# One zeroed tile for four masks, and a selector summed by TensorE, in a decode kernel that streams 54 MB

## The chip, the cores and the metric

The kernel runs on one core of a Trainium2 chip. The metric is the device time of one execution in microseconds. Beside the time, every execution has a span: from its first to its last instruction in the profile. The difference of the two is the time outside the span. All executions quoted here are recorded as of the fast state. The three sets of experiments ran on three different chips, each with the kernel before beside it; its time outside the span was 1.97 to 1.98 us on all three, so this quantity is compared across sets. A ratio is the mean time of one kernel's fast runs over that of the other's fast runs of the same rounds, so it is not quite the ratio of the medians that are quoted beside it.

## The reference

The reference mixes two branches for one token: attention over the last 4096 cached keys of 16 key/value heads, and a gelu MLP.

```python
g = sigmoid((x * gate_w).sum(-1, keepdims=True))
a = attention(x, k_cache[..., -4096:, :], v_cache[..., -4096:, :], wq, wo)   # 32 query heads, Dh 128
b = gelu(x @ w1 + b1) @ w2 + b2                                              # 576 -> 4608 -> 576
return g * a + (1 - g) * b
```

Each weight and each cached row in the window is used once, so the kernel reads 53.6 MB for very little arithmetic.

## The kernel before

All large transfers are issued by SyncE into five big buffers, in the order w1, wq, four key tiles, two value tiles, half of w2, and the rest of the values, wo and w2. GpSimd builds small masks at the start, while the weights come in. Four of them concern us: `perm` (it permutes the query heads), `lo31` (it selects row p mod 31), and `om_t` and `wo_tail`, which must be zero where nothing is written later.

```python
perm = const.tile([P, 4, 4, 32], BF16, name="perm")
nc.gpsimd.memset(perm[:], 0.0)
nc.gpsimd.affine_select(out=perm[:], in_=perm[:], ...)
hi5 = const.tile([P, 5], FP32, name="hi5")
nc.gpsimd.memset(hi5[:], 1.0)
# ... two selects on hi5
lo31 = const.tile([P, RW], BF16, name="lo31")            # RW = 31
nc.gpsimd.memset(lo31[:], 0.0)
for a in range(5):                                       # ones where p - 31 a == r
    nc.gpsimd.affine_select(out=lo31[:], in_=lo31[:], pattern=[[-1, RW]], base=-RW * a, ...)
om_t = const.tile([P, 64], BF16, name="om_t")
nc.gpsimd.memset(om_t[:], 0.0)
wo_tail = const.tile([48, 4, D], BF16, name="wo_tail")
nc.gpsimd.memset(wo_tail[:].bitcast(FP32), 0.0)
# ... more masks, last of all qz_flat
```

Near the end the attention output of each head is scaled by the gate over the softmax sum, masked into four groups of rows (`om`) and a tail (`om_t`), and re-laid by a product with the selector:

```python
rgh = ...   # rg x gh[:, 0:4], VectorE
rgt = ...   # rg x gh[:, 4],   VectorE, one more instruction
om, om_t = o_ps * rgh, o_ps * rgt
ov_mm = nc.tensor.matmul(ov_ps[:, 0:RO], lhsT=om, rhs=lo31[:], start=True, stop=True)
ov_mm = nc.tensor.matmul(ov_ps[0:64, RO:RO+4], lhsT=om_t, rhs=lo31[:, 0:4], start=True, stop=True)
```

GpSimd's program has 63 instructions and VectorE's 63, by the count that the change goes by. The trace records 60 and 59 of them, and 2230 of TensorE's; the differences between kernels are the same in both counts.

Of the kernel before, what the change touches and what calls it, by code (L numbers as in the profile page):

```python
# [9 lines left out]
FP32 = mybir.dt.float32  # L10
BF16 = mybir.dt.bfloat16
I32 = mybir.dt.int32
ACT = mybir.ActivationFunctionType
ALU = mybir.AluOpType
# [4 lines left out]
def kernel(  # L19
# [15 lines left out]
    nc = tc.nc  # L35

    P = 128
    D = 576
    Hq, Hkv, Dh = 32, 16, 128
# [126 lines left out]
    const = ctx.enter_context(tc.tile_pool(name="const", bufs=1))  # L166
# [36 lines left out]
    for base, pattern, keep in (  # L203
# [4 lines left out]
        n = 1  # L208
# [8 lines left out]
        out=is0[:], in0=low[:], scalar1=0.0, scalar2=None, op0=ALU.is_equal  # L217
    )
    alt = is0[:, 0 : 2 * NI].rearrange("p (i t) -> p i t", t=2)
    ones = const.tile([P, P], FP32, name="ones")  # L220
    nc.gpsimd.memset(ones[:], 1.0)
    ident = const.tile([P, P], BF16, name="ident")
    make_identity(nc, ident[:])
    perm = const.tile([P, 4, 4, 32], BF16, name="perm")
    nc.gpsimd.memset(perm[:], 0.0)
    nc.gpsimd.affine_select(
        out=perm[:],
        in_=perm[:],
        pattern=[[-64, 2], [-1, 2], [0, 4], [-2, 32]],
        compare_op=ALU.not_equal,  # L230
        fill=1.0,
        base=0,
        channel_multiplier=1,
    )
    RW = 31
    hi5 = const.tile([P, 5], FP32, name="hi5")
    nc.gpsimd.memset(hi5[:], 1.0)
    nc.gpsimd.affine_select(
        out=hi5[:],
        in_=hi5[:],  # L240
        pattern=[[-RW, 5]],
        compare_op=ALU.is_ge,
        fill=0.0,
        base=0,
        channel_multiplier=1,
    )
    nc.gpsimd.affine_select(
        out=hi5[:],
        in_=hi5[:],
        pattern=[[RW, 5]],  # L250
        compare_op=ALU.is_ge,
        fill=0.0,
        base=RW - 1,
        channel_multiplier=-1,
    )
    lo31 = const.tile([P, RW], BF16, name="lo31")
    nc.gpsimd.memset(lo31[:], 0.0)
    for a in range(5):
        nc.gpsimd.affine_select(
            out=lo31[:],  # L260
            in_=lo31[:],
            pattern=[[-1, RW]],
            compare_op=ALU.not_equal,
            fill=1.0,
            base=-RW * a,
            channel_multiplier=1,
        )
    om_t = const.tile([P, 64], BF16, name="om_t")
    nc.gpsimd.memset(om_t[:], 0.0)
    wo_tail = const.tile([48, 4, D], BF16, name="wo_tail")  # L270
    nc.gpsimd.memset(wo_tail[:].bitcast(FP32), 0.0)
    c0 = 2 * NI
    hi16 = const.tile([P, 16], FP32, name="hi16")
    nc.gpsimd.tensor_scalar(
        out=hi16[:], in0=is0[:, c0 : c0 + 16], scalar1=-SCALE, scalar2=None, op0=ALU.mult
# [5 lines left out]
        out=row_of[:],  # L281
        in_=row_of[:],
        pattern=[[0, 16], [-1, HB], [0, 2]],
        compare_op=ALU.not_equal,
        fill=1.0,
        base=0,
        channel_multiplier=1,
# [4 lines left out]
        out=foreign[:],  # L292
        in_=foreign[:],
        pattern=[[0, P], [-1, HB]],
        compare_op=ALU.not_equal,
        fill=0.0,
        base=0,
        channel_multiplier=1,
# [4 lines left out]
        out=xdup.rearrange("p (d t) -> p d t", t=2),  # L303
        in_=x_row.rearrange("p (d o) -> p d o", o=1).to_broadcast([1, D, 2]),
    )
    xs_ps = ps_m.tile([P, NI, 1], FP32, name="xs_ps", tag="m")
    for i in range(NI):
        nc.tensor.matmul(  # L308
            xs_ps[:, i, :],
            lhsT=xdup[:, i : 2 * D : NI],  # L310
            rhs=one_b[0:1, 0:1],
            start=(i == 0),
            stop=(i == NI - 1),
# [4 lines left out]
        out=x2[:], in0=xs_ps[:].to_broadcast([P, NI, 2]), in1=alt, op=ALU.mult  # L318
# [5 lines left out]
        out=junk_row,  # L324
        in0=x_row,
        in1=gw_row,
        scale=1.0,
        scalar=0.0,
        op0=ALU.mult,
# [12 lines left out]
        out=omg[:], in0=g_t[:], scalar1=-1.0, scalar2=1.0, op0=ALU.mult, op1=ALU.add  # L342
# [3 lines left out]
        out=b2g[:], in0=b2_row, scalar1=omg[0:1, 0:1], scalar2=None, op0=ALU.mult  # L346
    )
    gh = const.tile([P, 1, 5], FP32, name="gh")
    nc.vector.tensor_scalar(
        out=gh[:, 0, :], in0=hi5[:], scalar1=g_t[:, 0:1], scalar2=None, op0=ALU.mult  # L350
# [22 lines left out]
    for j in range(NJ):  # L373
        nc.tensor.matmul(
            h_ps[:, j:NF:NJ],
            lhsT=b1_t[:, j:FH:NJ],
            rhs=ident[0:2, 0:2],
            start=(j == 0),
            stop=False,
# [5 lines left out]
    for i in range(NI):  # L385
        for j in range(NJ):
            nc.tensor.matmul(  # L387
                h_ps[:, j:NF:NJ],
                lhsT=w1_t[:, i, j:FH:NJ],
                rhs=x2[:, i, :],  # L390
                start=False,
                stop=(i == NI - 1 and j == NJ - 1),
# [9 lines left out]
        out=poly[:],  # L402
        in0=z2[:],
        scalar1=2.0 * C0 * 0.044715,
        scalar2=2.0 * C0,
        op0=ALU.mult,
# [11 lines left out]
        out=gt[:], in0=hacc[:], scalar=omg[:, 0:1], in1=r_t[:], op0=ALU.mult, op1=ALU.mult  # L418
# [4 lines left out]
    for i in range(NI):  # L423
        for j in range(Hq // 2):
            nc.tensor.matmul(  # L425
                q_ps[:, j : Hq : Hq // 2],
                lhsT=wq_t[:, i, j * Dh : (j + 1) * Dh],
                rhs=x2[:, i, :],
                start=(i == 0 and j == 0),
                stop=(i == NI - 1 and j == Hq // 2 - 1),  # L430
# [5 lines left out]
    for j in range(4):  # L436
        nc.tensor.matmul(
            qj_ps[:, j, :, :].rearrange("p g q -> p (g q)"),
            lhsT=perm[:, j, :, :].rearrange("p b l -> p (b l)"),
            rhs=q_b[:],  # L440
            start=True,
            stop=True,
        )
    for b in range(4):
# [6 lines left out]
            out=diag[:, :, :, 0:8],  # L451
            in_=qj_ps[quad].rearrange("p j g q -> p g j q"),
# [140 lines left out]
    for u in range(2):  # L593
        load_tail = nc.sync.dma_start(
            out=wo_tail[32 * u : 32 * u + 16].rearrange("h j n -> h (j n)"),
            in_=wo_src[16 * u : 16 * u + 16, 4 * RW : P, :].rearrange("h j n -> h (j n)"),
        )
        four_engines.append(load_tail.ins.name)
    o_ps = ps_m.tile([P, Hq, 1], FP32, name="o_ps", tag="m")

    def value_products(g):
        for c in range(NCK):
# [16 lines left out]
        out=ls[:],  # L619
        in0=same8[:, 0:8].rearrange("p (o q) -> p o q", o=1).to_broadcast([P, NG, 8]),  # L620
        in1=sums[:].to_broadcast([P, NG, 8]),
        op=ALU.mult,
# [6 lines left out]
            t_ps, lhsT=ones[:], rhs=ls[:].rearrange("p g q -> p (g q)"), start=True, stop=True  # L629
        ),  # L630
    )
    rg = const.tile([P, Hq, 1], FP32, name="rg")
    nc.vector.reciprocal(out=rg[:, :, 0], in_=t_ps)  # L633
    rgh = const.tile([P, Hq, 4], FP32, name="rgh")
    nc.vector.tensor_tensor(
        out=rgh[:],
        in0=rg[:].to_broadcast([P, Hq, 4]),
        in1=gh[:, :, 0:4].to_broadcast([P, Hq, 4]),
        op=ALU.mult,
    )  # L640
    rgt = const.tile([P, Hq], FP32, name="rgt")
    nc.vector.tensor_scalar(
        out=rgt[:], in0=rg[:, :, 0], scalar1=gh[:, 0, 4:5], scalar2=None, op0=ALU.mult
    )
    queue("pe", lambda: value_products(3))

# [1 line left out]
    RO = RW  # L648
    wo_t = big.tile([P, RO, D], BF16, name="wo_t", tag="D")
    for r0, r1 in ((0, 16), (16, RO)):  # L650
        nc.sync.dma_start(  # L651
            out=wo_t[:, r0:r1, :].rearrange("p r n -> p (r n)"),
            in_=wo_src[:, 0 : 4 * RW, :].rearrange("h (a r) n -> h a (r n)", a=4)[
                :, :, r0 * D : r1 * D
            ],
        )
    for j0, j1 in ((0, 10), (10, 16), (16, 18)):
        nc.sync.dma_start(out=w2_t[:, NJ + j0 : NJ + j1, :], in_=w2_src[:, 1, j0:j1, :])  # L658

    om = const.tile([P, Hq, 4], BF16, name="om")  # L660
    nc.vector.tensor_tensor(  # L661
        out=om[:], in0=o_ps[:].to_broadcast([P, Hq, 4]), in1=rgh[:], op=ALU.mult
    )
    with tc.issue_after(issued["pe"].ins):
        for f in range(6):
            y_add(gt[:, f : f + 1], w2_t[:, f, :])
    nc.vector.tensor_tensor(
        out=om_t[:].rearrange("p (u h) -> p u h", u=2)[:, :, 0:16],
        in0=o_ps[:, :, 0].rearrange("p (u h) -> p u h", u=2),
        in1=rgt[:].rearrange("p (u h) -> p u h", u=2),  # L670
        op=ALU.mult,
    )
    ov_ps = ps_m.tile([P, RO + 4], FP32, name="ov_ps", tag="m")
    ov_mm = nc.tensor.matmul(
        ov_ps[:, 0:RO],
        lhsT=om[:].rearrange("p h a -> p (h a)"),
        rhs=lo31[:],
        start=True,
        stop=True,
    )  # L680
    with tc.issue_after(ov_mm.ins):
        ov_mm = nc.tensor.matmul(
            ov_ps[0:64, RO : RO + 4], lhsT=om_t[:], rhs=lo31[:, 0:4], start=True, stop=True
        )
    ov = const.tile([P, RO], BF16, name="ov")
    nc.vector.tensor_copy(out=ov[:], in_=ov_ps[:, 0:RO])
    ov_tail = const.tile([48, 4], BF16, name="ov_tail")
# [46 lines left out]
```

## Time and profile before

| | before |
|---|---|
| time, median of the runs beside the change | 132.34 us |
| profiled execution: time, span, difference | 132.28, 130.28, 2.00 us |
| read from HBM | 53.62 MB |
| GpSimd's masks end at | 17.49 us |
| the 864 KB of w2 that the chain names landed at | 127.39 us |
| the last 288 KB of w2 landed at | 128.07 us |

The table is read from the bottom up: the weights that the chain names land at 127.4 us, the last products, two casts and a store take the 2.9 us that follow, and two more microseconds lie outside every instruction. The lines of the profile stand in the prediction.

### The profile page before, as it was taken

Reading aid. Unit: us, or ns where it says so; the run is one execution under the profiler, and the core shown is the slowest. Engines: PE = TensorE matmul, PEld = TensorE weight load, DVE = VectorE, ACT = ScalarE, POOL = GpSimd, SP = SyncE. Lnnn points to the kernel's source line nnn. Section 1 sums busy time; section 2 is a strip of 40 time slices with the busy share of each in tenths; the row PEclk is TensorE's granted clock in tenths of the full one; section 3 lists DMA queues with packets and bytes.
Section 4 is the critical chain, followed back from the end, with each engine's and each line's share of the span. In section 5 each row is a group of like instructions: output and inputs, shape, how many; then the busy total and the mean of one; then the engine's idle time right before and its main releaser. Section 6 shows DMA issues by size and latency. Waiting matters only on the chain.

```text
span 130.3 us, 2411 instructions
## 1 busy us (share of the span) xinstructions
PE 80.7 (62%) x1145; PEld 46.1 (35%) x1077; DVE 53.7 (41%) x49; ACT 8.3 (6%) x18; POOL 10.1 (8%) x34
## 2 busy tenths in 40 slices
PE   0036999476003998949909995985300930899973
PEld 0036949475000121202201121685300920864641
DVE  0056100300079969999999995604000020010001
ACT  3000000003000000030003003021000000000001
POOL 5029930000000000000000000000000000000000
PEclk9999999999999999999996899975555555555999
DMA  7999999899999899899999999899999999999980
GB/s 232 421 436 439 468 401 498 363 463 438 392 448 463 372 453 483 372 443 473 392 433 463 412 412 463 376 444 473 397 423 448 423 407 421 430 427 421 403 354 25
DMA packets 2508, 53.75 MB, mean 413 GB/s; under 512 B 286, under 2 KB 290, under 8 KB 580
## 3 DMA queue, kind: packets, MB, share of 16 engines
q1 hardware_dynamic: 2490, 53.61, 96.5%
q8 instruction: 8, 0.13, 0.4%
q10 hardware_dynamic: 10, 0.01, 0.0%
HBM read 53.62 MB, written 0.00 MB: 412 GB/s over the span
## 4 chain that ended last, share of the span: by engine, by line
DMA 52%; DVE 24%; PE 14%; issue 6%; SPq 2%
DMA k_t<-in_A_k_cache_dram 27%; DMA w_t<-in_B_w_dram 25%; DVE kt L494 19%; PE s_ps L516 7%; PE o_ps L603 5%; DVE m L532 3%; DVE pt L565 2%; PE y_ps L359 1%; SPq L651 1%; DVE mr L535 1%; SPq L658 0%; SPq L194 0%; PE mt_ps L541 0%; DVE out_row L702 0%; SPq L190 0%
## 5 line engine op out<-in xcount | busy, mean ns | idle before, releaser
L516 PE MATMUL s_ps<-kt,qz_flat 128*128 128x512 bf16 x128 | 32.6, 412 | 17.2 <-DVE kt L494 10.4
L494 DVE STREAM_TRANSPOSE kt<-k_t 128x4096 f32<-128x4096 f32 x8 | 35.3, 4432 | 11.7 <-DMA k_t<-in_A_k_cache_dram 10.3
L603 PE MATMUL o_ps<-pt,v_t 128*128 128x8 bf16 x512 | 14.2, 167 | 16.8 <-DMA v_t<-in_A_v_cache_dram 14.8
L516 PEld LDWEIGHTS <-qz_flat 128*128 128x128 bf16 x64 | 6.8, 107 | 40.3 <-issue 40.2
L603 PEld LDWEIGHTS <-v_t 128*128 128x128 bf16 x512 | 14.1, 102 | 17.5 <-DMA v_t<-in_A_v_cache_dram 15.1
L387 PEld LDWEIGHTS <-w_t 128*128 128x128 bf16 x162 | 10.2, 165 | 0.9 <-issue 0.9
L387 PE MATMUL h_ps<-x,w_t 128*128 128x2 bf16 x162 | 10.4, 202 | 0.0
L359 PE MATMUL y_ps<-w_t,gt 128*1 128x288 bf16 x72 | 7.2, 363 | 1.2 <-DMA w_t<-in_B_w_dram 1.2
L553 ACT ACTIVATE p_t<-s_ps,negm 128x1024 bf16<-128x1024 f32 x4 | 4.5, 1113 | 50.9 <-DVE negm L549 50.9
L633 DVE RECIPROCAL rg<-mt_ps 128x32 f32<-128x32 f32 x1 | 0.4, 358 | 15.5 <-PE mt_ps L628 15.5
L565 DVE STREAM_TRANSPOSE pt<-p_t 128x1024 bf16<-128x1024 bf16 x4 | 4.9, 1224 | 2.7 <-ACT p_t L553 2.7
L425 PE MATMUL q_ps<-x,wq_t 128*128 128x2 bf16 x144 | 4.0, 166 | 2.7 <-DMA wq_t<-in_A_wq_dram 2.7
L702 DVE CAST out_row<-y_ps 1x288 bf16<-1x288 f32 x1 | 0.4, 445 | 11.7 <-PE y_ps L359 11.7
L308 PE MATMUL xs_ps<-one_b,rows 1*128 1x1 bf16 x9 | 0.7, 195 | 7.4 <-DVE rows L302 7.4
L532 DVE TENSOR_REDUCE m<-s_ps 128x1 f32<-128x1024 f32 x4 | 4.8, 1196 | 1.1 <-PE s_ps L516 1.1
L359 PEld LDWEIGHTS <-gt 128*1 128x1 bf16 x72 | 3.7, 99 | 3.6 <-issue 1.6
L425 PEld LDWEIGHTS <-wq_t 128*128 128x128 bf16 x144 | 3.9, 104 | 2.8 <-DMA wq_t<-in_A_wq_dram 2.8
L396 DVE COPY hacc<-h_ps 128x36 f32<-128x36 f32 x1 | 0.2, 196 | 10.6 <-PE h_ps L387 10.6
L359 PE MATMUL y_ps<-wo_t,ov 128*1 128x288 bf16 x62 | 4.3, 286 | 0.2 <-DMA wo_t<-in_A_wo_dram 0.2
L661 DVE TENSOR_TENSOR om<-o_ps,rgh 128x128 bf16<-128x128 f32 x1 | 0.3, 292 | 8.8 <-PE o_ps L603 8.8
L302 DVE COPY rows<-rows 1x1152 bf16<-1x1152 bf16 x1 | 0.7, 748 | 6.5 <-DMA rows<-in_A_x_dram 6.5
L359 PEld LDWEIGHTS <-ov 128*1 128x1 bf16 x62 | 2.6, 83 | 1.8 <-issue 0.8
(77 smaller groups left out, 39.1 us busy)
## 6 DMA issues: line engine op xcount, KB each, us to landing
k_t<-in_A_k_cache_dram SPq DMA_DIRECT2D x4, 4096.0 KB, 31.8
v_t<-in_A_v_cache_dram SPq DMA_DIRECT2D x4, 4096.0 KB, 23.2
wq_t<-in_A_wq_dram SPq DMA_DIRECT2D x1, 4608.0 KB, 25.8
w_t<-in_B_w_dram SPq DMA_DIRECT2D x1, 2880.0 KB, 14.2
w_t<-in_B_w_dram SPq DMA_DIRECT2D x1, 2592.0 KB, 23.1
w_t<-in_B_w_dram SPq DMA_DIRECT2D x1, 2304.0 KB, 8.1
wo_t<-in_A_wo_dram SPq DMA_DIRECT2D x1, 2304.0 KB
wo_t<-in_A_wo_dram SPq DMA_DIRECT2D x1, 2160.0 KB
```

Of the source, the lines that this page charges most:

```text
L302: nc.vector.tensor_copy(out=xdup.rearrange("p (d t) -> p d t", t=2), in_=x_row.rearrange("p (d o) -> p d o", o=1).to_broadcast([1, D, 2]),)
L359: last = nc.tensor.matmul(y_out[s], lhsT=vec, rhs=row[:, s * DH : (s + 1) * DH], start=start, stop=stop, skip_group_check=True,)
L387: nc.tensor.matmul(h_ps[:, j:NF:NJ], lhsT=w1_t[:, i, j:FH:NJ], rhs=x2[:, i, :], start=False, stop=(i == NI - 1 and j == NJ - 1), skip_grou ...
L425: nc.tensor.matmul(q_ps[:, j : Hq : Hq // 2], lhsT=wq_t[:, i, j * Dh : (j + 1) * Dh], rhs=x2[:, i, :], start=(i == 0 and j == 0), stop=(i ...
L494: lambda: nc.vector.transpose(out=kt[g, f][:].bitcast(FP32), in_=keys.rearrange("p c d -> p (c d)").bitcast(FP32),),
L516: last = nc.tensor.matmul(s_ps[g][:, u * 512 : (u + 1) * 512].rearrange("p (c k) -> p c k", k=32), lhsT=qz(g, j, 2 * f + half), rhs=kv[:, ...
L532: queue("dve", lambda: nc.vector.reduce_max(out=m1[:], in_=s_ps[g][:], axis=AX.X))
L535: lambda: nc.vector.tensor_scalar(out=mr[:], in0=hi16[:], scalar1=m1[:, 0:1], scalar2=None, op0=ALU.mult),
L553: nc.scalar.activation(out=p_t[:].rearrange("p c k -> p (c k)"), in_=s_ps[g][:], func=ACT.Exp, bias=negm[:, 0:1], scale=SCALE, accum_out=s ...
L565: lambda: nc.vector.transpose(out=pt[:, g, :, :].rearrange("p c q -> p (c q)"), in_=p_t[:].rearrange("p c k -> p (c k)"),),
L603: last = nc.tensor.matmul(o_ps[:, 8 * g : 8 * g + 8, 0], lhsT=v_t[g][:, c, :], rhs=pt[:, g, c % 32, 8 * (c // 32) : 8 * (c // 32) + 8], st ...
L651: nc.sync.dma_start(out=wo_t[:, r0:r1, :].rearrange("p r n -> p (r n)"), in_=wo_src[:, 0 : 4 * RW, :].rearrange("h (a r) n -> h a (r n)", ...
```

## The change

Its intent is to shorten two engines' programs: GpSimd from 63 to 51 instructions, VectorE from 63 to 62. The four zeroed tiles become parts of one, so one memset serves. The five selects that filled `lo31` one after the other become one select on five separate selectors (`at31`), and TensorE adds their products up in PSUM. VectorE makes five columns of `rgh` at once instead of four and one.

```diff
-    perm = const.tile([P, 4, 4, 32], BF16, name="perm")
-    nc.gpsimd.memset(perm[:], 0.0)
+    RW = 31
+    NZ = 512 + 5 * RW + 1 + 64
+    zeros = const.tile([P, NZ + 4 * D], BF16, name="zeros")
+    nc.gpsimd.memset(zeros[:].bitcast(FP32), 0.0)
+    perm = zeros[:, 0:512].rearrange("p (j b l) -> p j b l", j=4, b=4)
+    at31 = zeros[:, 512 : 512 + 5 * RW].rearrange("p (a r) -> p a r", a=5)
+    om_t = zeros[:, NZ - 64 : NZ]
+    wo_tail = zeros[0:48, NZ : NZ + 4 * D].rearrange("p (j n) -> p j n", j=4)
 ... select on perm as before
+    nc.gpsimd.affine_select(out=at31, in_=at31, pattern=[[-RW, 5], [-1, RW]], ...)
     hi5 = const.tile([P, 5], FP32, name="hi5")
-    nc.gpsimd.memset(hi5[:], 1.0)
     nc.gpsimd.affine_select(
-        in_=hi5[:],
+        in_=ones[:, 0:5],
 ...
-    lo31, its memset and its five selects; om_t, wo_tail and their memsets
 ...
-    rgh = const.tile([P, Hq, 4], FP32, name="rgh")
+    rgh = const.tile([P, Hq, 5], FP32, name="rgh")
 ...
-    rgt and its tensor_scalar
 ...
+    ov_mm = nc.tensor.matmul(
+        ov_ps[0:64, RO : RO + 4], lhsT=om_t, rhs=at31[:, 4, 0:4], start=True, stop=True
+    )
+    for a in range(4):
+        with tc.issue_after(ov_mm.ins):
+            ov_mm = nc.tensor.matmul(
+                ov_ps[:, 0:RO],
+                lhsT=om[:].rearrange("p h a -> p (h a)"),
+                rhs=at31[:, a, :],
+                start=(a == 0),
+                stop=(a == 3),
+            )
```

More of the change, by code (lines that the diff above doesn't have):

```diff
@@ L223 @@
     make_identity(nc, ident[:])
-    perm = const.tile([P, 4, 4, 32], BF16, name="perm")
-    nc.gpsimd.memset(perm[:], 0.0)
+    RW = 31
[6 more added lines that the diff above has]
+    wo_tail = zeros[0:48, NZ : NZ + 4 * D].rearrange("p (j n) -> p j n", j=4)
     nc.gpsimd.affine_select(
-        out=perm[:],
-        in_=perm[:],
+        out=perm,
+        in_=perm,
         pattern=[[-64, 2], [-1, 2], [0, 4], [-2, 32]],
@@ L234 @@
     )
-    RW = 31
+    nc.gpsimd.affine_select(
+        out=at31,
+        in_=at31,
+        pattern=[[-RW, 5], [-1, RW]],
+        compare_op=ALU.not_equal,
+        fill=1.0,
+        base=0,
+        channel_multiplier=1,
+    )
     hi5 = const.tile([P, 5], FP32, name="hi5")
-    nc.gpsimd.memset(hi5[:], 1.0)
     nc.gpsimd.affine_select(
         out=hi5[:],
-        in_=hi5[:],
+        in_=ones[:, 0:5],
         pattern=[[-RW, 5]],
@@ L255 @@
     )
-    lo31 = const.tile([P, RW], BF16, name="lo31")
-    nc.gpsimd.memset(lo31[:], 0.0)
-    for a in range(5):
-        nc.gpsimd.affine_select(
-            out=lo31[:],
-            in_=lo31[:],
-            pattern=[[-1, RW]],
-            compare_op=ALU.not_equal,
-            fill=1.0,
-            base=-RW * a,
-            channel_multiplier=1,
-        )
-    om_t = const.tile([P, 64], BF16, name="om_t")
-    nc.gpsimd.memset(om_t[:], 0.0)
-    wo_tail = const.tile([48, 4, D], BF16, name="wo_tail")
-    nc.gpsimd.memset(wo_tail[:].bitcast(FP32), 0.0)
     c0 = 2 * NI
@@ L633 @@
     nc.vector.reciprocal(out=rg[:, :, 0], in_=t_ps)
-    rgh = const.tile([P, Hq, 4], FP32, name="rgh")
+    rgh = const.tile([P, Hq, 5], FP32, name="rgh")
     nc.vector.tensor_tensor(
         out=rgh[:],
-        in0=rg[:].to_broadcast([P, Hq, 4]),
-        in1=gh[:, :, 0:4].to_broadcast([P, Hq, 4]),
+        in0=rg[:].to_broadcast([P, Hq, 5]),
+        in1=gh[:].to_broadcast([P, Hq, 5]),
         op=ALU.mult,
-    )
-    rgt = const.tile([P, Hq], FP32, name="rgt")
-    nc.vector.tensor_scalar(
-        out=rgt[:], in0=rg[:, :, 0], scalar1=gh[:, 0, 4:5], scalar2=None, op0=ALU.mult
     )
@@ L661 @@
     nc.vector.tensor_tensor(
-        out=om[:], in0=o_ps[:].to_broadcast([P, Hq, 4]), in1=rgh[:], op=ALU.mult
+        out=om[:], in0=o_ps[:].to_broadcast([P, Hq, 4]), in1=rgh[:, :, 0:4], op=ALU.mult
     )
@@ L667 @@
     nc.vector.tensor_tensor(
-        out=om_t[:].rearrange("p (u h) -> p u h", u=2)[:, :, 0:16],
+        out=om_t.rearrange("p (u h) -> p u h", u=2)[:, :, 0:16],
         in0=o_ps[:, :, 0].rearrange("p (u h) -> p u h", u=2),
-        in1=rgt[:].rearrange("p (u h) -> p u h", u=2),
+        in1=rgh[:, :, 4].rearrange("p (u h) -> p u h", u=2),
         op=ALU.mult,
@@ L674 @@
     ov_mm = nc.tensor.matmul(
-        ov_ps[:, 0:RO],
-        lhsT=om[:].rearrange("p h a -> p (h a)"),
-        rhs=lo31[:],
-        start=True,
-        stop=True,
-    )
-    with tc.issue_after(ov_mm.ins):
-        ov_mm = nc.tensor.matmul(
-            ov_ps[0:64, RO : RO + 4], lhsT=om_t[:], rhs=lo31[:, 0:4], start=True, stop=True
-        )
+        ov_ps[0:64, RO : RO + 4], lhsT=om_t, rhs=at31[:, 4, 0:4], start=True, stop=True
+    )
+    for a in range(4):
[7 more added lines that the diff above has]
+            )
     ov = const.tile([P, RO], BF16, name="ov")
```

## The prediction

> **What bounds the kernel now.** I read the page's forty slices first, then the table by stage, then the chain that ended last, and last the timelines of the two places that the change touches: GpSimd's masks at the start, and the last 16 us.
>
> In the slices each digit of the DMA row is a busy share in tenths, and GB/s is what was moved:
>
> ```profile
> DMA  7999999899999899899999999899999999999980
> GB/s 232 421 436 439 468 401 498 363 463 438 392 448 463 372 453 483 372 443 473 392 433 463 412 412 463 376 444 473 397 423 448 423 407 421 430 427 421 403 354 25
> HBM read 53.62 MB, written 0.00 MB: 412 GB/s over the span
> ```
>
> The DMA row has no hole except at its two ends. The table by stage is sharper (each engine's busy time, then the granted clock, the DMA share and GB/s):
>
> ```profile
> 37.00:60.00 23.00, 16.31 (x66) 3.58 (x34) 21.55 (x8) 1.20 (x2) 0.00 (x0) 1.00 1.01 432
> 90.00:105.00 15.00, 6.19 (x220) 6.11 (x217) 0.00 (x0) 0.00 (x0) 0.00 (x0) 0.50 1.00 427
> 115.00:122.00 7.00, 6.81 (x64) 3.29 (x62) 0.47 (x3) 0.15 (x1) 0.00 (x0) 0.61 1.01 427
> ```
>
> The DMA share is 1.00 whether VectorE is busy nearly throughout (37 to 60 us) or idle (90 to 105 us). The queue never runs dry, so the bytes fix the end. An estimate from these rows: 53.62 MB / 430 GB/s = 124.7 us of transfer, plus some 2 us before the stream is up and the 2.9 us after it (below), makes 129.6 us, against a span of 130.3.
>
> The end of the chain that ended last (start, length, what):
>
> ```profile
> 93.68 0.58 SPq L658
> 94.27 0.04 issue
> 94.31 33.08 DMA w_t<-in_B_w_dram
> 127.39 0.04 issue
> 127.44 1.19 PE y_ps L359 x16
> 128.62 0.43 DVE out_row L702
> ```
>
> The last weights are issued at 94.31 and land 33.08 us later, not because they are large (864 KB) but because they stand behind some 33 us of queue. That is why I don't trust the earlier part of this chain, which puts 24% of the span on VectorE: VectorE releases the buffers from which later transfers are issued, but each is issued long before the transfers ahead of it are done. A faster VectorE or GpSimd only lengthens the queue. What follows the last byte, 16 matmuls, two casts and a store of 1.1 KB (130.3 - 127.4 = 2.9 us), is untouched by the change.
>
> [...] 427 to 432 GB/s in the stages above, at a share of 1.00[...]. [...] The trace has 991 ns for a memset of 128x1084 fp32, 0.91 ns an element with everything[...]. [...] The page here shows 8 instruction packets of 0.13 MB in all, 16 KiB each, 0.4% of the DMA time[...]. [...]
>
> **GpSimd's part.** Here is what it does (start, length, then the instruction):
>
> ```profile
> 1.86 0.52 POOL L225 MEMSET perm<- 128x512 bf16 x1
> 9.05 0.62 POOL L216 TENSOR_SCALAR is<-low 128x162 f32<-128x162 int32 x1 [6.67 <-DVE low L214]
> ...
> 10.58 0.11 POOL L237 MEMSET hi<- 128x5 f32 x1
> 10.62 0.13 POOL L257 MEMSET lo<- 128x31 bf16 x1
> 10.68 0.15 POOL L269 MEMSET om_t<- 128x64 bf16 x1
> 10.76 1.05 POOL L271 MEMSET wo_tail<- 48x1152 f32 x1
> 11.77 0.41 POOL L238 TENSOR_SCALAR_AFFINE_SELECT hi<-hi 128x5 f32<-128x5 f32 x1
> ...
> 16.50 0.99 POOL L384 MEMSET qz_flat<- 128x1084 f32 x1
> ```
>
> - Added: the one zeroed tile, 732 + 2304 = 3036 bf16 columns, so 1518 as fp32: 1518 x 0.91 = 1.4 us. It replaces the perm memset at 1.86, in a wait that lasts until 9.05: 0.9 us more, at no cost.
> - Removed after 9.05: the memsets of hi5, lo31, om_t and wo_tail, by their distance from start to start 0.04 + 0.06 + 0.09 + 1.01 = 1.2 us; and the five selects of lo31, 0.21 us each but by their place between others 0.30 + 4 x 0.17 = 1.0 us, moves included.
> - Added after 9.05: one select of 128x155. From the selects of 128x128 (0.29 us) and 128x512 (0.745 us): 0.29 + 27 x 0.0012 = 0.32 us.
> - Sum: GpSimd ends 1.2 + 1.0 - 0.3 = 1.9 us earlier, at about 15.6 instead of 17.49 us; its busy time falls from 10.1 to about 9 us (0.9 - 0.1 - 0.1 - 0.15 - 1.05 - 1.05 + 0.3 = -1.25).
>
> What hangs on it? TensorE waits 0.96 us at 17.6 us for the memset of qz_flat, in the midst of the products with w1. These could end 1 us earlier, at 23.3 instead of 24.3 us. The query products then start when wq lands, and not before:
>
> ```profile
> 27.01 4.00 PE L425 MATMUL q_ps<-x,wq_t 128*128 128x2 bf16 x144 [2.69 <-DMA wq_t<-in_A_wq_dram]
> ```
>
> The wait of 2.69 us becomes 3.7 us, and the microsecond is lost again. Released a little earlier is also the third key transfer (issued at 24.35, when w1 has been read), but the first two are queued until 46 us. **Worth: 0.0 us.**
>
> **VectorE's part.** rgh has 5 columns instead of 4, 292 ns to an estimated 292 x 5/4 = 365 ns at most; rgt, 235 ns, goes. Net 0.16 us less at 105.9 us, where VectorE then waits 8.8 us for the last value products. **Worth: 0.0 us.**
>
> **TensorE's part.** One matmul of 128x31 becomes four on the same weights; the tail's 128x4 goes first, so it now waits for om_t, the second of two VectorE results. Here the places are:
>
> ```profile
> 116.31 0.21 PE L674 MATMUL ov_ps<-lo,om 128*128 128x31 bf16 x1
> 116.45 0.21 PE L682 MATMUL ov_ps<-lo,om_t 128*64 128x4 bf16 x1
> 116.59 2.49 PEld L359 LDWEIGHTS <-gt 128*1 128x1 bf16 x24
> 116.70 0.19 DVE L686 CAST ov<-ov_ps 128x31 bf16<-128x31 f32 x1 [1.43 <-PE ov_ps L682]
> ```
>
> om_t is done at 115.3, a microsecond before TensorE gets there, so the order costs nothing. The two matmuls start 0.14 us apart, so three more are 3 x 0.14 = 0.4 us at most. The pile of products behind them waits for DMA three times before the end: 0.19 us (121.9), 0.85 us (125.35) and 0.33 us (127.44). 0.4 us eats the first and 0.2 us of the second; the last wait stays. **Worth: 0.0 us.** The sum of all three parts is 0.0 us.
>
> **The rivals.**
> 1. *Launch and end.* The timed run of the profiled execution took 132.28 us for a span of 130.3, so 2.0 us lie outside it. If shorter programs shortened that part, the span would stay and the time would fall. No view can show it. That the change counts its instructions (51 and 62) speaks for it a little[...]. I put 20% on 0.3 to 1 us: 131.3 to 132.0.
> 2. *A wait through the shared tile.* om_t, wo_tail and the selector now share a tile. Were dependences kept by whole tile, VectorE's write of om_t at 115.1 us would wait for the load of wo_tail, and the load for the masks' readers. The load is issued at 80.2 with v_t behind it, and the last v_t lands at 111.3; so it has landed by then, and 0 us follows. A dependence of the load on a later reader would be a deadlock, not a delay.
> 3. *TensorE as the bound at the end.* The granted clock is 0.50 from 90 us on. If the added matmuls cost 0.4 us each at this clock, 1.2 us, they would just about use up the 1.37 us of waits: 0 to 0.2 us more, 132.5.
> 4. *A gain through the issue of transfers.* Earlier masks could let transfers start sooner. Against it: share 1.00 in every middle stage. At most the 0.1 us by which the slices fall short.
>
> **Range and chances.** With 0.0 us as the sum, the time would be 132.3; the 20% for rival 1 pulls it to 132.2. Downwards the range takes most of rival 1 in (131.4), upwards rival 3 and the spread of runs (132.6). Two per cent are 2.6 us, more than all that lies outside the span: faster 0.02, within 2% 0.97, slower 0.01.
>
> **What would show it.** Right: a span of 130.2 to 130.4, the DMA share 1.00 in the middle stages, the last weights landing at 127.3 to 127.5, GpSimd's last memset ending near 15.6, TensorE's wait for wq grown to about 3.7 us, and the wait at 125.35 shrunk by about 0.2 us. Wrong: a last landing that moves by over 0.3 us; no wait before the last 16 products; or a span that stays while the time changes, which would be rival 1.

## The result, and the profile after

The changed kernel took 131.95 us (median of 4 runs, 131.92 to 132.12) against 132.34 us for the kernel before: a ratio of 0.9973, interval 0.9955 to 0.999. A second set of six runs, with the first experiments, was closer: 132.04 against 132.12 us, 0.9995 (0.9979 to 1.0012), which is not clear of 1. By the two sets the change gains some 0.1 to 0.4 us, well within 2%; what is steadier is the part outside the span, below.

The profiled execution took 131.92 us and its span is 130.18 us. Before it was 132.28 and 130.28. Of the 0.36 us, then, 0.10 lie inside the span and 0.26 outside it.

The DMA row of the changed kernel's slices, and three rows of its table by stage (as before: busy times, granted clock, DMA share, GB/s):

```profile
DMA  7999999799899999999999999899999999999980
```

```profile
37.00:60.00 23.00, 16.21 (x67) 3.55 (x34) 21.84 (x8) 1.21 (x2) 0.00 (x0) 1.00 1.00 430
90.00:105.00 15.00, 6.03 (x218) 5.94 (x214) 0.00 (x0) 0.00 (x0) 0.00 (x0) 0.50 0.99 425
115.00:122.00 7.00, 6.59 (x69) 3.30 (x64) 0.39 (x3) 0.16 (x1) 0.00 (x0) 0.66 0.99 420
```

The queue is as full as before, and the end of the chain has moved by a tenth:

```profile
95.27 32.02 DMA w_t<-in_B_w_dram
127.29 0.04 issue
127.33 1.19 PE y_ps L356 x16
128.52 0.43 DVE out_row L696
```

These weights were issued 0.96 us later than before (95.27 against 94.31) and yet landed 0.1 us earlier (and so did the last 288 KB, 127.97 against 128.07). That is what a full queue looks like: here the moment of issue did not matter.

GpSimd, from the changed kernel's timeline (start, length, instruction):

```profile
1.87 1.36 POOL L227 MEMSET zeros<- 128x1518 f32 x1
8.98 0.62 POOL L216 TENSOR_SCALAR is<-low 128x162 f32<-128x162 int32 x1 [5.75 <-DVE low L214]
10.52 0.59 POOL L241 TENSOR_SCALAR_AFFINE_SELECT zeros<-zeros 128x155 bf16<-128x155 bf16 x1
...
14.70 0.99 POOL L381 MEMSET qz_flat<- 128x1084 f32 x1
```

The masks end at 15.69 instead of 17.49 us, and nothing came of it. Two lines of the kernel before, then two of the changed kernel, show why. PE is the matmul row and PEld the weight-load row of the same engine:

```profile
16.56 1.12 PE L359 MATMUL y_ps<-b2g,ones 1*1 1x288 f32 x4
17.61 0.10 PEld L503 LDWEIGHTS <-row_of 4*128 4x128 bf16 x1 [0.96 <-POOL qz_flat L384]
```

```profile
15.44 1.12 PE L356 MATMUL y_ps<-b2g,ones 1*1 1x288 f32 x4
16.48 1.14 PEld L384 LDWEIGHTS <-w_t 128*128 128x128 bf16 x17 [0.96 <-issue]
```

The gap of 0.96 us before a weight load is there in both, behind the same four fp32 products, which take 1.12 us. It is the weight-load row that has nothing to do while the matmul row is busy. The memset of qz_flat had merely ended within that gap before the change, and so got its name. The products with w1 end at 24.4 us in both kernels, and the query products wait for wq just as long:

```profile
27.05 4.00 PE L422 MATMUL q_ps<-x,wq_t 128*128 128x2 bf16 x144 [2.71 <-DMA wq_t<-in_A_wq_dram]
```

One thing more differs beside the new masks. VectorE's scaling of the bias row (1x576, fp32 out) took 1,757 to 1,762 ns in the three profiled kernels with the old masks (before, b4, c3), beside memsets of GpSimd, and 575 to 580 ns in the ten with the new ones, beside a select. Which instruction of the old masks did it was not tested.

In the last 16 us the added products are these:

```profile
116.21 0.21 PE L667 MATMUL ov_ps<-zeros 128*64 128x4 bf16 x1
116.36 0.29 PE L672 MATMUL ov_ps<-zeros,om 128*128 128x31 bf16 x4
116.58 3.07 PE L356 MATMUL y_ps<-w_t,gt 128*1 128x288 bf16 x24
```

Five products take the place of two, and the next ones start at 116.58 against 116.60 us. Four products of 31 columns on the same weights take 0.29 us together.

What the profile's pages do not show is in the trace's records of DMA packets: packets of 8 KiB that belong to the instruction queue 14, before and after the program. The kernel before has one that starts after the span:

```
kernel     queue  start (us from the span's start)  length  bytes
before     14     132.033                           0.531   8192      (span 130.283)
after      none after 0
```

The changed kernel's trace has no such packet, in either of its two profiles. Queue 8 has eight packets of 16 KiB in both kernels, all inside the span; that they fetch TensorE's program is inferred, since it has 2230 recorded instructions and the next longest 60. This made the theory to test: **a fetch of instructions at the very end**, which a shorter program does without.

### The profile page after: what moved, and what is told of

Read it like the earlier page. It is cut to its first block, busy times and chain, and to the rows that moved or that the text cites. A ratio compares the mean times of both kernels' runs of the same rounds, so it can differ in the third digit from the quotient of the medians.

```text
span 130.2 us, 2401 instructions
## 1 busy us (share of the span) xinstructions
PE 80.3 (62%) x1148; PEld 46.2 (35%) x1077; DVE 52.3 (40%) x48; ACT 8.3 (6%) x18; POOL 9.2 (7%) x26
## 4 chain that ended last, share of the span: by engine, by line
DMA 60%; DVE 21%; PE 9%; issue 6%; SPq 2%; DVEq 0%
DMA k_t<-in_A_k_cache_dram 31%; DMA w_t<-in_B_w_dram 25%; DVE kt L491 15%; PE o_ps L600 5%; DMA rows<-in_A_x_dram 4%; PE s_ps L513 3%; DVE m L529 3%; DVE pt L562 2%; SPq L644 2%; PE y_ps L356 1%; DVE mr L532 1%; SPq L651 0%; PE mt_ps L538 0%; DVE out_row L696 0%; DVE negm L546 0%
```

## The experiments

Three theories were put against each other. Theory G: the length of GpSimd's program sets the time outside the span. Theory V: VectorE's does. Theory W: the change gained by doing less work. Later G became S (a step, a fetch that is there or not) against L (a price for each instruction). Programs were lengthened with memsets of two elements each on a scratch tile, in early waits of the engine:

```diff
+    pad_g = const.tile([1, 2 * n], BF16, name="pad_g")
+    for k in range(n):
+        nc.gpsimd.memset(pad_g[:, 2 * k : 2 * k + 2], 0.0)     # pad_v, nc.vector: before w1_t
     RW = 31
```

Here is what all of them gave. "Outside" is the mean of time less span over the runs (the spans are recorded to 0.1 us). "Packet" is the start of the 8 KiB packet that came last: with a sign relative to the span's end, with "at" from the span's start; from one profile of each.

| run | GpSimd, VectorE | median us | ratio (interval) | mean span | outside | packet |
|---|---|---|---|---|---|---|
| before, 33 runs in three sets | 63, 63 | 132.12, 132.27, 132.14 | | 130.17, 130.28, 130.20 | 1.97, 1.98, 1.97 | +1.75 |
| after, first set | 51, 62 | 131.95 | 0.9973 (0.9955 to 0.999) | 130.25 | 1.74 | none |
| a0_after_again | 51, 62 | 132.04 | 0.9995 (0.9979 to 1.0012) | 130.25 | 1.83 | none |
| a1_gpsimd63 | 63, 62 | 132.39 | 1.0019 (1.0008 to 1.0031) | 130.10 | 2.30 | +2.12 |
| a2_vector63 | 51, 63 | 131.91 | 0.998 (0.9967 to 0.9993) | 130.08 | 1.79 | +1.71 |
| a3_both63 | 63, 63 | 132.21 | 1.0011 (0.9998 to 1.0023) | 130.28 | 1.96 | +1.73 |
| b1_gpsimd57 | 57, 62 | 132.16 | 0.9995 (0.9982 to 1.0008) | 130.38 | 1.81 | none |
| b2_gpsimd62 | 62, 62 | 132.58 | 1.0021 (1.0007 to 1.0036) | 130.28 | 2.26 | +2.12 |
| b3_gpsimd75 | 75, 62 | 132.48 | 1.0021 (1.0009 to 1.0033) | 130.58 | 1.95 | +0.24 |
| b4_vector_part | 63, 62 | 132.65 | 1.0028 (1.0016 to 1.004) | 130.30 | 2.32 | +2.13 |
| c1_gpsimd99 | 99, 62 | 132.11 | 0.9994 (0.9981 to 1.0007) | 130.36 | 1.73 | at 6.6 us |
| c2_vector98 | 51, 98 | 132.22 | 1.0017 (0.9996 to 1.0038) | 130.72 | 1.67 | at 51.4 us |
| c3_before_padded | 99, 99 | 132.21 | 1.0002 (0.999 to 1.0014) | 130.60 | 1.59 | at 15.5 and 50.3 us |
| c4_bias16 | 51, 62 | 131.83 | 0.9978 (0.9966 to 0.999) | 130.14 | 1.73 | none |

The column "outside" is far steadier than the times. The 33 runs of the kernel before lie between 1.91 and 2.02 us. Nine of the ten runs of the changed kernel lie between 1.71 and 1.80, and one, of the second set, at 2.26, which stays unexplained. That one and two long spans (130.4, 130.5) are what made the second set's ratio so poor.

The profiles show one thing more about the packet. Where it starts over 1 us after the span, its end can be set beside the time outside the span of the same execution:

```
                 packet ends   outside   difference   (us)
before              2.28         2.00       0.28
a1_gpsimd63         2.67         2.37       0.30
a2_vector63         2.11         1.82       0.29
a3_both63           2.24         1.98       0.26
b2_gpsimd62         2.67         2.38       0.29
b4_vector_part      2.66         2.36       0.30
```

The packet took 0.40 to 0.55 us, and the difference keeps to 0.26 to 0.30 us. This is what one would see if the execution ended with that fetch. It is an agreement of six profiles and not an experiment on the packet itself, and the constant 0.3 us is unexplained.

### a0_after_again: the control

> The changed kernel once more, as the control of the three runs beside it. Every theory: 131.9 to 132.0 us (ratio to before 0.997), a span of about 130.2, so 1.75 us outside the span.

The median of 132.04 us is 0.1 us over what was expected, for the reason just given. The profile has a span of 130.17 us and again no packet after the end.

### a1_gpsimd63: GpSimd's program back at its old length

> The changed kernel with 12 memsets of two elements each added to GpSimd in its early wait (3.3 to 9 us), where nothing waits for them: GpSimd has 63 instructions again, VectorE keeps 62. Theory G (the time outside the span depends on the length of GpSimd's program): back to 132.3 us, span 130.2, 2.0 us outside, and the 8 KiB instruction packet after the end of the span is back. Theory V (VectorE's length): 131.9. Theory W (what was saved is work inside the span, such as the 0.1 us by which the stream ended earlier): 131.9.

The time went to 132.39 us, the span did not grow (130.10), and the packet after the end came back. The work inside the span is that of the changed kernel, so theory W cannot explain it; theory G held. The 2.30 us outside are more than the 2.0 expected, though, and the packet came later than before the change (+2.12 against +1.75).

### a2_vector63: VectorE's program back at its old length

> The changed kernel with one memset of two elements added to VectorE before its first wait: VectorE has 63 instructions again, GpSimd keeps 51. Theory V: 132.3 us and the trailing packet is back. Theory G: 131.9, no trailing packet. Theory W: 131.9.

The packet is back, at +1.71 us, but the time is 131.91 us: theory V's time did not come. Outside the span it is 1.79 us, four runs at 1.84 to 1.90 and two at 1.60 to 1.62. Theory G missed too, since it had expected no packet. A packet after the end alone does not make the run much longer: this one ended at 2.11 us, and the 1.82 us outside in that profile are 0.08 more than without any. Why two runs lie below 1.7 is open.

### a3_both63: both at their old length

> Both additions: 63 and 63 instructions as before the change, but the work of the changed kernel. Theories G and V: 132.3 us; if each program costs a part of it, a1 and a2 lie between 131.9 and 132.3 and this is their sum. Theory W: 131.9.

Outside the span: 1.96 us, as before the change (1.97), with the packet at +1.73 as before (+1.75). So the two lengths alone bring back the old value, with none of the old work. But the prices do not add up: GpSimd's 12 instructions cost 0.56 us with VectorE at 62 and 0.17 with VectorE at 63. Why is open; only one packet after the end was seen even where both programs have 63.

### b1_gpsimd57 and b2_gpsimd62: a step or a slope

> The changed kernel with 6 memsets of two elements added to GpSimd in its early wait: 57 instructions, VectorE 62. So far the time outside the span (time less span) was 1.73 us with 51 and 62, 2.30 with 63 and 62, 1.79 with 51 and 63, 1.96 with 63 and 63 (as before the change, 1.97). Theory S (a step: an 8 KiB instruction packet after the end that is there or not): 1.73 and no packet after the end, or 2.3 with one, nothing between. Theory L (each instruction of GpSimd costs its share): 1.73 + 6 x 0.57 / 12 = 2.0 us. The span 130.1 to 130.3 by both.

> The changed kernel with 11 added memsets: GpSimd 62, VectorE 62. Theory S: 1.73 us outside the span if the step lies between 62 and 63 as it does for VectorE's packet, 2.3 if it lies lower, with a packet after the end in that case alone. Theory L: 2.25 us.

With 57 instructions four of five runs lie at 1.72 to 1.76 us outside, one at 2.06, and no packet came after the end. (The time was no better than before the change all the same, since the span was 130.38 us where 130.1 to 130.3 was expected.) With 62, five of six lie at 2.24 to 2.42, one at 1.95, and the packet was there at +2.12. Outside the span six added instructions cost next to nothing (four of the five runs) and eleven cost 0.5 us: a step between 57 and 62. Theory L would have had 2.0 and 2.25; the second number is met by both theories, so it is b1, and b3 below, that speak against L.

### b3_gpsimd75: further up

> The changed kernel with 24 added memsets: GpSimd 75, VectorE 62. Theory S: as with 63, 2.3 us outside the span and a packet after the end, or back to less if the packet comes early enough by then. Theory L: 1.73 + 24 x 0.0475 = 2.87 us, so 133.0 us in all.

With more instructions the time outside fell to 1.95 us and the packet came at +0.24. Theory L's 2.87 is far off. But the span grew to 130.58 us on average, and the trace shows where: in GpSimd's own end section, which no view of the page counts as work.

```
GpSimd, start in us      before     b3_gpsimd75
semaphore update         129.696    129.660
drain                    129.776    130.075
first range clear        129.882    130.331
last range clear         130.061    130.514
```

Between the update and the next drain 0.08 us passed before the change, and 0.42 us here. In the trace of the kernel before, this drain names no semaphore to wait for. This stall lengthens the span by 0.3 us. My estimate was that GpSimd waits there for the fetch. The trace does not bear it out: the packet starts at 130.78 us, 0.7 us after the drain that ends the stall. The stall's cause is open. So are the 1.95 us outside, since this packet had ended 0.77 us after the span's end.

### b4_vector_part: one part of the change alone

```diff
-    rgh = const.tile([P, Hq, 4], FP32, name="rgh")
+    rgh = const.tile([P, Hq, 5], FP32, name="rgh")
 ... rgt and its tensor_scalar taken out of the kernel before
```

> The kernel before with VectorE's part of the change alone (rgh with five columns, no rgt): GpSimd 63, VectorE 62. Theory G (the program lengths set the time outside the span, as in the run with 12 added memsets): 2.3 us outside, so 132.4 to 132.6, not faster than before. Theory W (the saved instructions count as work): 131.9 to 132.3.

The part that only takes an instruction away made the kernel slower, by 0.3%: 132.65 us, ratio 1.0028, an interval clear of 1. The span is the old one (130.30 against 130.28), and outside it are 2.32 us, as in a1 with the same two lengths. This is the sharpest result of the set: at equal lengths (63 and 62) two kernels with different masks agree to 0.03 us outside the span, and both differ from 63 and 63.

### c1_gpsimd99, c2_vector98 and c3_before_padded: the fetch moved into the span

> The changed kernel with 48 added memsets: GpSimd 99, VectorE 62. With 57 instructions there was no packet after the end and 1.74 us outside the span; with 62 and 63 one came 2.12 us after the span's end, 2.26 to 2.32 us outside; with 75 it came 0.24 us after, 1.95 us outside, and GpSimd's last instructions stood still for 0.3 us. Theory S (the fetch costs only where it falls at the end of GpSimd's program): with 99 the fetch comes before the end section, hidden, no packet after the end, 1.74 us outside and a span of 130.2, so 131.95 us although 48 instructions were added. Theory L (each instruction has its price): over 2.3 us outside, 132.5 or more.

> The changed kernel with 36 memsets of two elements added to VectorE before its first wait: VectorE 98, GpSimd 51. Theory S carried over to VectorE: no packet after the end, 1.7 us outside the span, 131.9 to 132.0. If VectorE's length has a price of its own, over 1.8 us outside.

> The kernel before with 36 useless memsets each on GpSimd and VectorE in their early waits (99 and 99 instructions instead of 63 and 63), else unchanged. Theory S: no packet after the end, 1.74 us outside the span, a ratio of 0.998 to the kernel before: as much as the change gained, by adding instructions. Theory W (the change gained by doing less): 132.3 or more, ratio 1.000 or above.

Outside the span theory S held in all three: 1.73, 1.67 and 1.59 us (the last 0.15 below what was expected), and no packet after the end. The kernel before, with 72 useless memsets and nothing else, loses 0.37 us outside its span (1.965 to 1.594), more than the change achieves there. The packets turned up inside, one for each lengthened program. The list of queues of c1_gpsimd99 and c3_before_padded (packets, MB, share) now has a line that the pages of before and after lack:

```profile
q14 instruction: 1, 0.01, 0.0%
```

```profile
q14 instruction: 2, 0.02, 0.0%
```

This also shows whose packets they are: 48 instructions more on GpSimd alone put one at 6.6 us, 36 more on VectorE alone put one at 51.4 us, and both together put one at 15.5 and one at 50.3 us. VectorE had begun 62 and 61 of its recorded instructions by then. GpSimd had begun 69 in c1 and 83 in c3, so its packet does not come at a fixed place of its program.

But the times did not follow: 132.11, 132.22 and 132.21 us against 132.14, since the spans grew by 0.16 to 0.5 us on average (in c2 one run of 131.4 us is in the mean). Theory S had expected 131.95 and a ratio of 0.998 for c1 and c3; that part failed, and the ratio of 1.0002 for c3 is one that theory W allowed. What speaks against W in c3 is the time outside the span alone. The trace's completion writes say something of the cause. Each transfer ends with sixteen of them; these are the last six of the last 288 KB of weights, in us (the landing is recorded 0.44 to 0.48 us after the last write, at 128.07 us in the kernel before):

```
before            127.31 127.32 127.39 127.44 127.58 127.58
after             127.34 127.35 127.39 127.44 127.47 127.53
c1_gpsimd99       127.29 127.30 127.34 127.37      127.73
c2_vector98       127.31 127.39 127.43 127.47      127.87
c3_before_padded  127.33 127.35 127.67 127.78      127.99
```

(The last three rows have their last five.) In c1 and c2 a single one of the sixteen parts is behind the rest by 0.36 and 0.40 us, and the packet inside took 0.31 and 0.33 us. Before and after have no such straggler. By the recorded landings the last of the sixteen is 0.36, 0.37 and 0.22 us behind the one before it in c1, c2 and c3, and at most 0.12 us in the other eleven profiles. My estimate, from these sizes alone, is that the fetch set one of the sixteen parts back by about its own length, and that this part decided the end in c1 and c2. The trace does not name the DMA engine of a packet, so this is not shown. b1 had a span 0.1 us longer than before without any such packet.

### c4_bias16: the gap behind the four fp32 products

```diff
-    b2g = const.tile([1, D], FP32, name="b2g")
+    b2g = const.tile([1, D], BF16, name="b2g")
-    y_add(ones[0:1, 0:1], b2g[0:1, :], start=True)
+    y_add(one_b[0:1, 0:1], b2g[0:1, :], start=True)
```

> The changed kernel with the output bias added in bf16 instead of fp32 (two bf16 products of 288 columns in place of four fp32 ones). In the profile of the change TensorE still stood still for 0.96 us after these four, although GpSimd's last memset was done 1.9 us earlier. Theory F (the fp32 products run on past the end that the profile gives them): the idle time behind them falls below 0.3 us and the products with w1 end about 1 to 1.5 us earlier than 24.4 us. Theory Q (something else holds TensorE there): it stays 0.96. By both 131.8 to 132.0 us, since the query weights land at 27.0 us all the same.

The expectation was itself still worded by a misreading: TensorE did not stand still there, the matmul row was busy. From this run's timeline:

```profile
14.65 0.40 PE L356 MATMUL y_ps<-b2g,one_b 1*1 1x288 bf16 x2
14.97 1.90 PE L384 MATMUL h_ps<-x,w_t 128*128 128x2 bf16 x28
...
26.88 1.28 PE L422 MATMUL q_ps<-x,wq_t 128*128 128x2 bf16 x42 [3.37 <-DMA wq_t<-in_A_wq_dram]
```

The bias now takes 0.40 us instead of 1.12, the gap in the weight-load row behind it is 0.25 us instead of 0.96 (the matmul row has none), and the products with w1 are read out at 23.55 us instead of 24.38. So the fp32 products were the 0.96 us, and not the masks. Of theory F's numbers the short gap came, but the products with w1 ended 0.83 us earlier and not 1 to 1.5; its mechanism, products that run on past their recorded end, is not needed. The 0.83 us gained are lost again in the wait for wq, 3.37 us now. The time is 131.83 us, with 1.73 outside the span: as good as the changed kernel, and faster than the kernel before by 0.22% (an interval clear of 1). It is not shown to be faster than the changed kernel.

## Why the prediction was right or wrong

The time of 131.95 us lies in the range of 131.4 to 132.6, and "within 2%" came. The sum of 0.0 us was right for the span. Outside the span it was not, and the time lies in the range because most of rival 1 had been let into it. Point by point:

- **The bound.** Right. The DMA share was 0.99 to 1.03 in every stage from 9 to 122 us, the last landing moved by 0.1 us, and the span is 130.18 us in the profile, where 130.2 to 130.4 was expected. Over the sets, the spans of before and after differ by less than they scatter. One reading was off: the 864 KB at 127.39 us are not the last byte (288 KB land at 128.07), which changes nothing here. Nor are 427 to 432 GB/s all that the table shows: the stage from 9 to 18 us has 441.
- **GpSimd's sum.** Right in its end: 15.69 us against 15.6, of which 0.07 us is only an earlier start (8.98 against 9.05). The zeroed tile took 1.36 us (estimate 1.4). The new select took 0.59 us, not 0.32.
- **"TensorE waits 0.96 us at 17.6 us for the memset of qz_flat".** This step failed. The products with w1 ended at 24.4 us as before, not at 23.3, and the wait for wq stayed at 2.71 us instead of growing to 3.7. The line that I read was the weight-load row's; its gap was the 1.12 us of the four fp32 products (c4). The worth of 0.0 us was right all the same, since the wait for wq swallows even a real gain of 0.83 us (c4).
- **VectorE's part.** Inside the span worth nothing, as said. Its real effect is on the program's length, and alone it is a loss of 0.36 us on average (b4).
- **TensorE's part and rival 3.** The three further products cost nothing that can be seen: the next products start at 116.58 against 116.60 us. Four took 0.29 us together; rival 3's 1.2 us did not come. The wait at 125 us was 0.83 us instead of 0.85, not 0.2 less. (The clock of 0.50 that rival 3 put down "from 90 us on" holds where the added products are, but not to the end: it is 1.00 from 122 us on.)
- **Rival 2.** No wait through the shared tile: VectorE writes om_t at 115.00 us, right behind om, as before (115.09).
- **Rival 1.** This is what came, and it was given 20%. The argument against it, that programs this short save no fetch, was the wrong step, and so was that no view could show it, since the trace's packets did: these engines' packets are 8 KiB, and the packet at the end came or went with a few instructions, between 57 and 62 on GpSimd and with the 63rd on VectorE. Its measured size is some 0.23 us of steady gain outside the span (1.97 to 1.74), a little under the 0.3 to 1 us that was put on it.

That the program lengths set the time outside the span is shown (a1, a3, b4). That they do it by way of the fetch is supported by where the packets lie and end, and not shown. Open are why the lengths 63 and 62 are worse than 63 and 63, and what exactly the engines do in the time outside the span.

## What to carry to other kernels

In this kernel, with a DMA share of 1.00 from 9 to 122 us, rearranging work on the compute engines was worth nothing inside the span: GpSimd was done 1.8 us earlier, and the products with w1 0.83 us earlier in c4. Look for a full queue first. The time outside the span is a quantity of its own: when a small change gives a few tenths that no view explains, subtract the span from the time and look for instruction packets after the last instruction. Here the price was a step: removing one instruction cost 0.34 us outside the span (b4), removing that one and twelve more gained 0.23, and adding 36 or 48 moved the packet into the span. Before calling a gap in the weight-load row a wait of TensorE, look at what the matmul row does in it.
